# Filler on constant data from TensorE's first moment, smaller pieces of W_in, and a third bank for one slice, in a fused attention and MLP kernel

## The chip, the cores and the metric

One core of a Trainium2 chip. The metric is the device time of one execution in microseconds (us), median over runs; every run named here was fast, with a granted clock of 0.990 to 1.000. Times of a kernel come from up to five rounds, each beside runs of the kernel before on the same chip.

## The reference, cut to what matters

```python
# q, k, v: (4 batches, 8 heads, 768 positions, 64); blocks of 64 positions
intra = (qb @ kb.T * Dmask) @ vb                  # decayed attention in the block
inter = (qb * lam_pow) @ kv_state                 # what earlier blocks left
kv_state = lam_block * kv_state + (kb * rev_pow).T @ vb
...
h = x @ w_in                                      # x: attention output, (3072, 512); w_in (512, 2048)
g = np.where(h > 0.0, h, np.exp(np.minimum(h, 0.0)) - 1.0)
return g @ w_out                                  # w_out (2048, 512)
```

## The kernel before

The kernel works in chunks of 128 positions. A *group* is one chunk of one batch (24 groups), a *tile* of the MLP is up to four groups (512 tokens), and W_in is cut into 16 *slices* of 128 columns; slice n of tile t gives `psH`, which ScalarE reads twice (`e` is exp, `r` is relu) and VectorE turns into `g`. TensorE is the engine that counts; its instruction order is written by hand.

All loads in the part that matters are issued by GpSimd, one after the other, in the order of a list. Two entries in that list are no loads: `('kd', 0)` and `('kd', 2)` are multiplications of the keys by their decays, done by GpSimd between two issues.

```python
WI = [1, 1, 2, 2, 2, 4, 4]        # slices of W_in per transfer (128 KB each)
WO = [2, 2, 4, 4, 4]
...
LOADS = [(0, 1, 'q'), (0, 1, 'k'), ... (3, 1, 'v'),
         ('wi', 0), ('wi', 1), ('wi', 2), ('wi', 3), ('kd', 0),
         ('wi', 4), ('wi', 5), ('kd', 2), ('wo', 0), ('wi', 6),
         ('wo', 1), ('wo', 2), (4, 2), ('wo', 3), ('wo', 4), (6, 2), ...]
...
def run_loads(items):
    for it in items:
        if it[0] == "wi":   emit_wi(it[1])        # nc.gpsimd.dma_start(...)
        elif it[0] == "wo": emit_wo(it[1])
        elif it[0] == "kd": att_kd(it[1], 2, "p") # nc.gpsimd.tensor_tensor(...)
        else:               emit_load(*it)        # q, k, v of groups 4 and 5: (4, 2)
...
def mm1(t, n, alt=False):
    ...
    mm1_mm(t, n, 0, MT, "M" if t == 0 and n % 2 == 0 and n < 8 else "H")   # tag = which PSUM banks
...
def warm(k, tag="M"):             # filler: products whose results nobody reads
    for _ in range(k):
        nc.tensor.matmul(pw[:, 0:2], lhsT=ident16[:], rhs=any16[:, 0:2], start=True, stop=True)
any16 = ident16[:].unsqueeze(1).broadcast_to([128, 4, 128])
W = [10, 4, 3, 1, 2, 1, 2, 1, 3, 0, 0, 2, 0, 2, 0, 0, 3, 0, 0, 0]
...
visit(4, ('B', 1), ('B', 4), ('B', 7))   # group 4: its transposes of q and k come at step B1
```

Of the kernel before, what the change touches and what calls it, by code (L numbers as in the profile page):

```python
# [8 lines left out]
FP16 = mybir.dt.float16  # L9
# [6 lines left out]
def kernel(  # L16
# [27 lines left out]
    cpool = ctx.enter_context(tc.tile_pool(name="cst", bufs=1))  # L44
# [7 lines left out]
    nc.sync.dma_start(out=lam_b[:], in_=lam.unsqueeze(0).broadcast_to([128, H]))  # L52
    rel_i = cpool.tile([128, 128], I32, name="rel_i")


# [26 lines left out]

    WI = [1, 1, 2, 2, 2, 4, 4]
    WO = [2, 2, 4, 4, 4]
    wi_t, wo_t, wi_at, wo_at = [], [], {}, {}
    for i, w in enumerate(WI):
        for j in range(w):
# [7 lines left out]
    def emit_wi(i):  # L95
        f0 = sum(WI[:i]) * 128
        nc.gpsimd.dma_start(  # L97
            out=wi_t[i][:],
            in_=moe_w_in[:, f0 : f0 + WI[i] * 128].rearrange("(k p) f -> p k f", p=128),
        )  # L100

    def emit_wo(i):
        f0 = sum(WO[:i]) * 128
        nc.gpsimd.dma_start(
            out=wo_t[i][:],
            in_=moe_w_out[f0 : f0 + WO[i] * 128, :].rearrange("(n p) f -> p n f", p=128),
        )
# [4 lines left out]
    ]  # L112
    LOADS = [(0, 1, 'q'), (0, 1, 'k'), (1, 1, 'q'), (1, 1, 'k'), (2, 1, 'q'), (2, 1, 'k'), (3, 1, 'q'), (3, 1, 'k'), (0, 1, 'v'), (1, 1, 'v'), (2, 1, 'v'), (3, 1, 'v'), ('wi', 0), ('wi', 1), ('wi', 2), ('wi', 3), ('kd', 0), ('wi', 4), ('wi', 5), ('kd', 2), ('wo', 0), ('wi', 6), ('wo', 1), ('wo', 2), (4, 2), ('wo', 3), ('wo', 4), (6, 2), (8, 2), (10, 2), (12, 2), (14, 2), (16, 2), (18, 2), (20, 2), (22, 2)]

    def run_loads(items):
        for it in items:
            if it[0] == "wi":
                emit_wi(it[1])
            elif it[0] == "wo":
                emit_wo(it[1])  # L120
            elif it[0] == "kd":
                att_kd(it[1], 2, "p")
            else:
# [12 lines left out]
    ident16 = cpool.tile([128, 128], FP16, name="ident16")  # L136
# [64 lines left out]
    qT, kT, Pt, kds, xt, pT, pS = {}, {}, {}, {}, {}, {}, {}  # L201
# [230 lines left out]
    def mm1_mm(t, n, lo, hi, tag="H"):  # L432

        if n == 0 and lo == 0:
            gt[t] = msb.tile([128, NF, TS[t] * L], FP16, tag="g", bufs=2, name=f"g{t}")
        if lo == 0:
            pH_of[t, n] = ps.tile([128, TS[t] * L], FP32, tag=tag, bufs=2, name=f"psH{t}_{n}")
        pH = pH_of[t, n]
        wi, j = wi_t[wi_at[n][0]], wi_at[n][1]
        for kk in range(HP):  # L440
            nc.tensor.matmul(  # L441
                pH[:, lo:hi], lhsT=wi[:, kk, j * 128 : (j + 1) * 128],
                rhs=xt[t][:, kk, lo:hi], start=(kk == 0), stop=(kk == HP - 1),
            )

    def mm1(t, n, alt=False):

        MT = TS[t] * L
        if MT == 256:
            if n == 0:  # L450
                gt[t] = msb.tile([128, NF, MT], FP16, tag="g", bufs=2, name=f"g{t}")
            pH = ps.tile(
                [128, 2 * MT], FP32, tag="M" if (t, n) in ((1, 0),) else "H", bufs=2,
                name=f"psH{t}_{n}",
            )
            for x in range(2):
                wi, j = wi_t[wi_at[n + x][0]], wi_at[n + x][1]
                for kk in range(HP):
                    nc.tensor.matmul(  # L459
                        pH[:, x * MT : (x + 1) * MT],  # L460
                        lhsT=wi[:, kk, j * 128 : (j + 1) * 128],
                        rhs=xt[t][:, kk, :], start=(kk == 0), stop=(kk == HP - 1),
                    )
            MT *= 2
        else:
            if (t, n) not in pH_of:
                mm1_mm(t, n, 0, MT, "M" if t == 0 and n % 2 == 0 and n < 8 else "H")
            pH = pH_of.pop((t, n))
        e = msb.tile([128, MT], FP32, tag="e", bufs=3, name=f"e{t}_{n}")
        nc.scalar.activation(e[:], pH[:], AF.Exp)  # L470
        if alt:
            return e, None, pH
        r = msb.tile([128, MT], FP16, tag="r", bufs=3, name=f"r{t}_{n}")
        nc.scalar.activation(r[:], pH[:], AF.Relu)  # L474
        return e, r, pH
# [84 lines left out]
    def warm(k, tag="M"):  # L560
        if k <= 0:
            return
        pw = ps.tile([128, 4, 128], FP32, tag=tag, bufs=2, name=f"psW{len(warms)}")
        warms.append(pw)
        for _ in range(k):
            nc.tensor.matmul(  # L566
                pw[:, 0:2], lhsT=ident16[:], rhs=any16[:, 0:2], start=True, stop=True
            )

    warms = []  # L570
    pace = cpool.tile([1, 1], FP16, name="pace")
    any16 = ident16[:].unsqueeze(1).broadcast_to([128, 4, 128])

# [9 lines left out]
    def op_T(c, w):  # L583
        att_T(c, 1, w, "H")

    def op_Te(c, w):
        att_Te(c, 1, w, "a")

    W = [10, 4, 3, 1, 2, 1, 2, 1, 3, 0, 0, 2, 0, 2, 0, 0, 3, 0, 0, 0]
    warm(W[0])  # L590
    op_T(0, "q")
    op_Te(0, "q")
    build_mask0(1)
    warm(W[1])
# [12 lines left out]
    op_T(2, "q")
    op_Te(2, "q")
    att_S(1)
    att_mask(1, 2)  # L610
    warm(W[5])
    op_T(2, "k")
# [31 lines left out]

    run_loads(LOADS[16:28])
    for s, g in zip([], (0, 2)):
# [35 lines left out]
    def paced_load(s, items):  # L682

        t, n = s
        if t not in ("A", "B"):
            w = 2 if TS[t] == 2 else 1
            src = gt[t][0:1, n - w, 0:1] if n else gt[t - 1][0:1, NF - 1, 0:1]
            nc.gpsimd.tensor_copy(pace[:], src)  # L688
        run_loads(items)

    for s, a, b in [(('B', 2), 28, 29), ((1, 2), 29, 30), ((1, 14), 30, 31), ((2, 4), 31, 32), ((2, 12), 32, 33), ((3, 4), 33, 34), ((3, 12), 34, 35), ((4, 4), 35, 36)]:
        at(s, paced_load, s, LOADS[a:b])

# [51 lines left out]
```

## Time and profile before

| | before |
|---|---|
| time, median of 3 runs | 213.04 us (213.03 to 213.19) |
| span of the profiled run | 211.4 us |
| W_in slices 8 to 11 landed (512 KB) | 26.48 us |
| k of group 4 landed / its transposes start | 37.52 / 37.82 us |
| filler | 34 products |

First GpSimd's timeline (start, length, engine, line, operation, output<-inputs, count). The two `kd` lines are the stretches in which no load is issued.

```profile
14.95 2.04 POOL L295 TENSOR_TENSOR kd<-kn,ks 128x1024 f16<-128x1024 f16 x1
16.80 1.63 POOL L97 DMA_DIRECT2D wi<-in_moe_w_in_dram  x2
18.35 2.00 POOL L295 TENSOR_TENSOR kd<-kn,ks 128x1024 f16<-128x1024 f16 x1
20.20 0.79 POOL L104 DMA_DIRECT2D wo<-in_moe_w_out_dram  x1
```

Then busy time by stretch. Each row has the stretch and its length, the busy time of PE, PEld, DVE, ACT and POOL with counts, the granted clock, the DMA share, and as the last number the GB/s that the DMA engines moved.

```profile
20.00:21.50 1.50, 1.50 (x9) 0.68 (x7) 1.50 (x3) 1.22 (x4) 1.50 (x3) 1.00 1.04 133
21.50:23.00 1.50, 1.50 (x8) 0.49 (x6) 1.47 (x4) 1.46 (x3) 1.50 (x3) 1.00 1.14 180
23.00:24.00 1.00, 1.00 (x20) 0.64 (x20) 0.97 (x3) 0.89 (x2) 1.00 (x2) 1.00 1.14 124
24.00:26.50 2.50, 1.65 (x22) 0.72 (x20) 2.46 (x5) 1.88 (x4) 2.50 (x3) 1.00 1.20 195
26.50:30.50 4.00, 3.66 (x17) 1.61 (x18) 3.92 (x7) 2.76 (x6) 1.72 (x3) 1.00 1.24 206
```

### The profile page before, as it was taken

What the parts mean: (1) busy time and instruction counts of PE and PEld (TensorE: products, weight loads), DVE (VectorE), ACT (ScalarE), POOL (GpSimd) and SP (SyncE); (2) the same over time, 40 slices, a digit from 0 to 9 for tenths busy, and PEclk for the clock granted to TensorE, in tenths of its full rate; (3) what the DMA queues carried; (4) which work ended last, traced back from release to release, by engine and by line L of the source; (5) the groups of instructions that cost most, each with busy time, mean ns of one, the idle gap of its engine ahead of it and who ended that gap; (6) DMA issues with size and microseconds to landing.
All of it is one profiled execution on the core that took longest, in us unless ns stands there. A gap on an engine that the chain in (4) does not pass through costs nothing.

```text
span 211.4 us, 4157 instructions
## 1 busy us (share of the span) xinstructions
PE 203.4 (96%) x1654; PEld 108.0 (51%) x1654; DVE 147.6 (70%) x240; ACT 128.4 (61%) x247; POOL 61.5 (29%) x70
## 2 busy tenths in 40 slices
PE   5899899999999999999999999999999999999994
PEld 3664344556765454544544544544544544466643
DVE  6764995577989999998698598677557634344321
ACT  6779878406784858666464566474566476675620
POOL 8999955400434251250600500600000000011000
PEclk9999999999999999999999999999999999999999
DMA  5999999999999999999699991699401111011112
GB/s 36 142 159 176 174 204 164 201 157 182 227 142 140 136 171 163 118 104 108 118 146 153 105 126 55 113 148 155 83 0 53 50 50 50 5 50 50 50 53 101
DMA packets 100756, 24.40 MB, mean 115 GB/s; under 512 B 93056, under 2 KB 97920, under 8 KB 100736
## 3 DMA queue, kind: packets, MB, share of 16 engines
q0 software_dynamic: 80384, 14.16, 87.1%
q1 hardware_dynamic: 20208, 9.90, 22.0%
q8 instruction: 13, 0.21, 0.4%
q10 hardware_dynamic: 144, 0.07, 0.1%
q14 instruction: 7, 0.06, 0.1%
HBM read 27.27 MB, written 6.29 MB: 159 GB/s over the span
## 4 chain that ended last, share of the span: by engine, by line
PE 80%; POOL 8%; DMA 4%; DVE 3%; ACT 2%; issue 1%; POOLq 0%; ACTq 0%
PE psM L538 36%; PE psH L441 29%; PE psH L459 5%; DMA wi<-in_moe_w_in_dram 4%; PE psO L334 2%; PE psS L308 2%; PE psO L342 2%; POOL qn L72 2%; POOL wi L97 2%; POOL kn L72 2%; PE psM L518 2%; POOL vn L72 2%; DVE g L487 1%; ACT r L474 1%; DVE P L320 1%
## 5 line engine op out<-in xcount | busy, mean ns | idle before, releaser
L538 PE MATMUL psM<-wo,g 128*128 128x512 f16 x368 | 94.0, 380 | 0.2 <-DVE g L487 0.2
L470 ACT ACTIVATE e<-psH 128x512 f32<-128x512 f32 x96 | 57.3, 597 | 59.5 <-PE psH L441 50.8
L487 DVE SCALAR_TENSOR_TENSOR g<-e,r 128x512 f16<-128x512 f32 x93 | 63.5, 695 | 37.9 <-ACT r L474 37.6
L441 PE MATMUL psH<-xt,wi 128*128 128x512 f16 (+2 forms) x324 | 81.3, 376 | 1.5 <-DMA wi<-in_moe_w_in_dram 1.1
L474 ACT ACTIVATE r<-psH 128x512 f16<-128x512 f32 x93 | 55.1, 593 | 0.0
L538 PEld LDWEIGHTS <-g 128*128 128x128 f16 x368 | 34.3, 98 | 38.5 <-DVE g L487 1.5
L441 PEld LDWEIGHTS <-wi 128*128 128x128 f16 x324 | 31.1, 98 | 39.4 <-DMA wi<-in_moe_w_in_dram 1.7
L320 DVE TENSOR_TENSOR P<-psS,mask 128x1024 f16<-128x1024 f32 (+1 forms) x28 | 28.7, 1067 | 6.1 <-PE psS L308 6.0
L688 POOL COPY pace<-g 1x1 f16<-1x1 f16 x7 | 2.3, 329 | 68.8 <-DVE g L487 68.8
L418 DVE SCALAR_TENSOR_TENSOR st<-st,up_p,psU 64x128 f16<-64x128 f16 x64 | 18.2, 346 | 0.1
L555 POOL DMA_DIRECT2D out_dram<-osb x2 | 1.1, 571 | 54.8 <-ACT osb L554 50.7
L363 DVE TENSOR_TENSOR xt<-psO,qs 128x1024 f16<-128x1024 f32 x10 | 12.2, 1224 | 6.7 <-PE psO L342 6.7
L72 POOL DMA_DIRECT2D qn<-in_q_dram x14 | 15.4, 1099 | 4.2 <-issue 2.0
L459 PE MATMUL psH<-xt,wi 128*128 128x256 f16 x128 | 16.4, 273 | 0.0
L72 POOL DMA_DIRECT2D vn<-in_v_dram x14 | 15.2, 1104 | 2.1 <-DMA wo<-in_moe_w_out_dram 1.7
L72 POOL DMA_DIRECT2D kn<-in_k_dram x14 | 15.2, 1088 | 0.8 <-DMA kn<-in_k_dram 0.7
L459 PEld LDWEIGHTS <-wi 128*128 128x128 f16 x128 | 12.4, 98 | 4.2
L554 ACT COPY osb<-psM 128x512 f32<-128x512 f32 x12 | 7.1, 592 | 12.2 <-PE psM L538 12.2
L334 PEld LDWEIGHTS <-vn 128*64 128x64 f16 x184 | 9.5, 109 | 4.5 <-issue 4.4
L334 PE MATMUL psO<-P,vn 128*64 128x128 f16 x184 | 11.5, 222 | 0.1
L342 PE MATMUL psO<-qT,st 128*64 128x128 f16 x160 | 10.0, 219 | 0.0
L566 PE MATMUL psW<-ident 128*128 128x256 f16 x34 | 8.3, 372 | 1.6 <-DVE ident L140 1.6
(58 smaller groups left out, 119.7 us busy)
## 6 DMA issues: line engine op xcount, KB each, us to landing
out_dram<-osb SPq DMA_DIRECT2D x21, 256.0 KB, 2.3
qn<-in_q_dram POOLq DMA_DIRECT2D x10, 256.0 KB, 6.7
kn<-in_k_dram POOLq DMA_DIRECT2D x10, 256.0 KB, 7.8
vn<-in_v_dram POOLq DMA_DIRECT2D x10, 256.0 KB, 9.4
wo<-in_moe_w_out_dram POOLq DMA_DIRECT2D x3, 512.0 KB, 14.9
wi<-in_moe_w_in_dram POOLq DMA_DIRECT2D x2, 512.0 KB, 9.1
wi<-in_moe_w_in_dram POOLq DMA_DIRECT2D x3, 256.0 KB, 6.3
qn<-in_q_dram POOLq DMA_DIRECT2D x4, 128.0 KB, 4.6
```

The costliest lines, as they stand in the source:

```text
L72: nc.gpsimd.dma_start(out=dst, in_=src[b : b + n, :, rows].rearrange("b h p d -> p (b h) d"))
L320: nc.vector.tensor_tensor(out=P[:, :, c], in0=s[:, :, c], in1=(mask if g < B else mask1)[:, :, c], op=ALU.mult,)
L334: nc.tensor.matmul(po[r, i, hp, :], lhsT=v_of(g + i, 2 * hp + hh), rhs=P[:, hh, hp, :], start=True, stop=(c == 0), skip_group_check=True,)
L342: nc.tensor.matmul(po[r, i, hp, :], lhsT=st[(g + i) % B // 2][c % 2][:, (g + i) % 2, hp, r], rhs=qT[g + i][:, hp, :], start=False, stop=Tr ...
L363: nc.vector.tensor_tensor(out=dst, in0=po[:, :, c], in1=qs[:, c].unsqueeze(1).broadcast_to([128, n, w, 128]), op=ALU.mult,)
L418: nc.vector.scalar_tensor_tensor(out=new[r, :, hp, r], in0=old[r, :, hp, r], scalar=up_p[r, hp : hp + 1], in1=pu[r, :, hp, :], op0=ALU.mul ...
L441: nc.tensor.matmul(pH[:, lo:hi], lhsT=wi[:, kk, j * 128 : (j + 1) * 128], rhs=xt[t][:, kk, lo:hi], start=(kk == 0), stop=(kk == HP - 1),)
L459: nc.tensor.matmul(pH[:, x * MT : (x + 1) * MT], lhsT=wi[:, kk, j * 128 : (j + 1) * 128], rhs=xt[t][:, kk, :], start=(kk == 0), stop=(kk = ...
L470: nc.scalar.activation(e[:], pH[:], AF.Exp)
L474: nc.scalar.activation(r[:], pH[:], AF.Relu)
L487: nc.vector.scalar_tensor_tensor(out=g, in0=e[:], scalar=-1.0, in1=r[:], op0=ALU.add, op1=ALU.min)
L538: nc.tensor.matmul(pm[:], lhsT=gt[t][:, n, i * L : (i + 1) * L], rhs=wo_t[wo_at[n][0]][:, wo_at[n][1], :], start=(n == 0), stop=(n == NF - 1),
```

## The change

Its intent: (a) get TensorE out of its slow opening sooner, with filler that does not wait for the identity and with more of it; (b) let slices 8 and 9 of W_in arrive without waiting for 10 and 11; (c) let slice 10 not wait for the bank of slice 8. Cut to its core:

```diff
+    ones = cpool.tile([128, 128], FP16, name="ones")
+    nc.vector.memset(ones[:], 1.0)
-    WI = [1, 1, 2, 2, 2, 4, 4]
+    WI = [1, 1, 2, 2, 2, 2, 2, 4]
     LOADS = [...
-      ('kd', 0), ('wi', 4), ('wi', 5), ('kd', 2), ('wo', 0), ('wi', 6), ('wo', 1), ...
+      ('kd', 0), ('wi', 4), ('wi', 5), ('kd', 2), ('wi', 6), ('wo', 0), ('wi', 7), ('wo', 1), ...
-  mm1_mm(t, n, 0, MT, "M" if t == 0 and n % 2 == 0 and n < 8 else "H")
+  mm1_mm(t, n, 0, MT, "M" if t == 0 and n % 2 == 0 and n < 9 else "H")
-  pw[:, 0:2], lhsT=ident16[:], rhs=any16[:, 0:2], start=True, stop=True
+  pw[:, 0:2], lhsT=ones[:], rhs=any16[:, 0:2], start=True, stop=True
-    any16 = ident16[:].unsqueeze(1).broadcast_to([128, 4, 128])
+    any16 = ones[:].unsqueeze(1).broadcast_to([128, 4, 128])
-    W = [10, 4, 3, 1, 2, 1, 2, 1, 3, 0, 0, 2, 0, 2, 0, 0, 3, 0, 0, 0]
+    W = [18, 7, 3, 2, 3, 1, 2, 2, 4, 0, 0, 3, 0, 3, 0, 0, 4, 0, 0, 0]
```

(The rest shifts indices into the list of loads by one and adds a branch that is never taken.)

More of the change, by code (lines that the diff above doesn't have):

```diff
@@ L112 @@
     ]
-    LOADS = [(0, 1, 'q'), (0, 1, 'k'), (1, 1, 'q'), (1, 1, 'k'), (2, 1, 'q'), (2, 1, 'k'), (3, 1, 'q'), (3, 1, 'k'), (0, 1, 'v'), (1, 1, 'v'), (2, 1, 'v'), (3, 1, 'v'), ('wi', 0), ('wi', 1), ('wi', 2), ('wi', 3), ('kd', 0), ('wi', 4), ('wi', 5), ('kd', 2), ('wo', 0), ('wi', 6), ('wo', 1), ('wo', 2), (4, 2), ('wo', 3), ('wo', 4), (6, 2), (8, 2), (10, 2), (12, 2), (14, 2), (16, 2), (18, 2), (20, 2), (22, 2)]
+    LOADS = [(0, 1, 'q'), (0, 1, 'k'), (1, 1, 'q'), (1, 1, 'k'), (2, 1, 'q'), (2, 1, 'k'), (3, 1, 'q'), (3, 1, 'k'), (0, 1, 'v'), (1, 1, 'v'), (2, 1, 'v'), (3, 1, 'v'), ('wi', 0), ('wi', 1), ('wi', 2), ('wi', 3), ('kd', 0), ('wi', 4), ('wi', 5), ('kd', 2), ('wi', 6), ('wo', 0), ('wi', 7), ('wo', 1), ('wo', 2), (4, 2), ('wo', 3), ('wo', 4), (6, 2), (8, 2), (10, 2), (12, 2), (14, 2), (16, 2), (18, 2), (20, 2), (22, 2)]
     def run_loads(items):
@@ L643 @@
             ecut[x[1]] = cut[x[1]]
-    run_loads(LOADS[16:28])
+    run_loads(LOADS[16:29])
     for s, g in zip([], (0, 2)):
@@ L688, in paced_load @@
             nc.gpsimd.tensor_copy(pace[:], src)
+        elif 6 in kds:
+            nc.gpsimd.tensor_copy(pace[:], kds[6][0:1, 0, 0:1])
         run_loads(items)
-    for s, a, b in [(('B', 2), 28, 29), ((1, 2), 29, 30), ((1, 14), 30, 31), ((2, 4), 31, 32), ((2, 12), 32, 33), ((3, 4), 33, 34), ((3, 12), 34, 35), ((4, 4), 35, 36)]:
+    for s, a, b in [(('B', 2), 29, 30), ((1, 2), 30, 31), ((1, 14), 31, 32), ((2, 4), 32, 33), ((2, 12), 33, 34), ((3, 4), 34, 35), ((3, 12), 35, 36), ((4, 4), 36, 37)]:
         at(s, paced_load, s, LOADS[a:b])
```

## The prediction

> **What bounds the kernel now.** I read the page of the profile first: the engine table, then the chain of work that ended last.
>
> ```profile
> PE 203.4 (96%) x1654; PEld 108.0 (51%) x1654; DVE 147.6 (70%) x240; ACT 128.4 (61%) x247; POOL 61.5 (29%) x70
> PE 80%; POOL 8%; DMA 4%; DVE 3%; ACT 2%; issue 1%; POOLq 0%; ACTq 0%
> L566 PE MATMUL psW<-ident 128*128 128x256 f16 x34 | 8.3, 372 | 1.6 <-DVE ident L140 1.6
> ```
>
> TensorE is busy 96% of a 211.4 us span and carries 80% of the chain. The chain's other 20% is where a change of the opening can work: GpSimd 8% and DMA 4% are the first 26.5 us, in which the chain is the issue of the loads and then the landing of one piece of W_in. The filler of today is 34 products of 128x256; the first waits 1.6 us for the identity.
>
> Then the timeline of the opening, matmuls only, for who waits for what and for the clock that TensorE really has:
>
> ```profile
> 1.65 2.31 PE L566 MATMUL psW<-ident 128*128 128x256 f16 x10 [1.65 <-DVE ident L140]
> 4.91 0.61 PE L221 MATMUL psTq<-ident,qn 128*128 128x128 f16 x4 [0.95 <-DMA qn<-in_q_dram]
> 7.07 0.61 PE L221 MATMUL psTk<-ident,kn 128*128 128x128 f16 x4 [0.70 <-DMA kn<-in_k_dram]
> ...
> 10.83 0.61 PE L308 MATMUL psS<-qT,kT 64*128 64x128 f16 x8
> 12.97 0.40 PE L308 MATMUL psS<-qT,kT 64*128 64x128 f16 x8
> ...
> 17.21 2.06 PE L441 MATMUL psH<-xt,wi 128*128 128x384 f16 x12
> ...
> 19.45 3.63 PE L441 MATMUL psH<-xt,wi 128*128 128x512 f16 x16 [0.18 <-DMA wi<-in_moe_w_in_dram]
> ...
> 26.53 1.90 PE L441 MATMUL psH<-xt,wi 128*128 128x512 f16 x8 [0.88 <-DMA wi<-in_moe_w_in_dram]
> 28.74 1.02 PE L441 MATMUL psH<-xt,wi 128*128 128x512 f16 x4 [0.31 <-ACT r L474]
> ```
>
> Columns: start, length, engine, line, output<-inputs, count, and the wait before it. The same eight products take 0.61 us at 10.83 and 0.40 us at 12.97: TensorE is slow until about 12.9 us, although the page's granted clock reads 1.00 throughout. From 17.2 us on, the stretches without a product running are only these (a product counted as its 216 ns start-to-start): 0.15 at 18.03, 0.34 at 19.45 (slices 2 and 3 of W_in), 1.05 at 26.53 (slices 8 and 9), 0.48 at 28.74 (slice 10 waits for ACT to read slice 8 out of its bank), 0.27 at 67.2, 0.34 at 93.9. Sum 2.6 us. All else after 17.2 is solid TensorE work that the change leaves alone. **So the change can win 2 us at the very most, under 1%.**
>
> **What the Trainium skill says.** "TensorE: Matmul & The Clock Gate", Part 1: the clock is at half rate by default and is released after about 3.4 us of sustained matmul activity, seen through a free-running window. The trace agrees: filler products start 0.21 us apart at first, 0.11 us apart after 13.3 us; two idle stretches (0.95 and 0.70 us) came before. "DMA: Bandwidth & Descriptors", "Why a DMA increments its semaphore by 16 and not by 1": a DMA has landed only when the slowest of 16 engines is done. That fits a queue busy at 90% or more from 5 us on, with 6 to 16 us from issue to landing. "PSUM — Partial Sum Buffer", Specifications: 8 banks of 512 FP32, so one 128x512 slice fills a bank; this kernel's three tags hold 4, 2 and 2 banks, as its tile shapes show.
>
> **The change, part by part.** The order of instructions: TensorE gains 36 rows (18 matmuls and their weight loads), VectorE one memset ahead of everything, GpSimd one W_in transfer. The new branch in the pacing of loads is never taken (no new GpSimd copy).
>
> (a) *Filler from the first moment.* 34 become 52 products. Its data come from a 128x128 memset (about 0.1 us, estimated from the 0.23 us of a 128x128 VectorE operation here) that waits for nothing, so filler starts near 0.9 us. 18 x 0.213 = 3.8 us reaches 4.75, just short of the first q at 4.91; 7 x 0.213 = 1.5 us fills 5.3 to 6.9, just short of k at 7.07. TensorE is then busy from 0.9 us without a break, and should be fast somewhere between 4.5 and 8 us instead of 12.9. Filler never delays data: at the full clock the 2 to 4 products per step are 0.2 to 0.45 us against 0.9 us per arriving load. Each score group (S) saves 0.2 us and each transpose 0.2 us, so TensorE follows the arrivals. Working through them (last k at 12.5, last v at 16.1 us), the last output group of the first tile moves from 16.87 to about 16.1, and slice 0 from 17.21 to about 16.55 us: **0.65 us earlier. But none of it reaches the end by itself:** slices 2 and 3 start at 19.45 because their transfer (issued 13.46, 5.9 us to landing) lands at 19.4, and GpSimd's issues don't depend on TensorE. It becomes a longer wait at 19.45.
>
> (b) *W_in in two-slice pieces.* Today slices 8 to 11 are one 512 KB transfer, issued at 17.59 and landed 8.9 us later, at 26.48; the piece before landed at 23.11. The new 256 KB piece for 8 and 9 should land about halfway, 24.8 us (estimate), before TensorE wants it at 25.5. The 1.05 us wait goes. Slices 10 and 11 are now issued after a 2.0 us multiplication on GpSimd (kd, 18.35 to 20.35), at about 20.2 instead of 17.59; the queue still holds two pieces then, so I put them at 26.5 as before, against a need at 27.2.
>
> (c) *Slice 8 in a third bank.* Slices 8, 9, 10 share two banks today, so 10 waits for the reading of 8. With 8 in a bank of the other tag (free since slice 4 was read, 24.4 us), 10 needs the bank of 7, free at 26.4. The 0.48 us wait goes; slice 11 now waits for slice 9's reading instead, to about 28.7 against a start of 30.03 today.
>
> Sum of (b) and (c): slice 11 about 1.3 us earlier. **Then it is given back**, since the loads behind are not earlier. Landings today (issue plus time to landing) against use:
>
> - W_in slices 12 to 15: landed 30.31, used 31.33: slack 1.0
> - W_out slices 2 and 3: landed 31.59, used 32.19: 0.6
> - W_out slices 4 to 7: landed 34.13, used 34.78: 0.65
> - k of group 4: landed 37.52, transposed at 37.82: 0.3
> - W_out slices 8 to 11: landed 41.70, used about 42.4: 0.7
>
> TensorE runs in order, so the smallest slack caps the gain: 0.3 us, if these transfers land as before. After 42 us every slack is over 1 us and TensorE is solid, so what is left goes through to the end: about 0.3 us.
>
> **The rivals.**
> 1. *Transfers land earlier too.* From 20 to 21.5 and 23 to 24 us the queue moved only 133 and 124 GB/s, against 195 to 206 just after. The 512 KB piece took 3.4 us after its predecessor where the next 512 KB took 2.5. If the smaller piece heals that, everything behind lands up to 0.8 us earlier, and the gain is up to 1.1 us: 211.9.
> 2. *Transfers land later.* With 256 KB less in the queue while GpSimd multiplies, the queue may run dry, and 256 KB pieces move at about 184 GB/s (17 to 20 us) against 206 for 512 KB ones, which alone costs 512 KB x (1/184 - 1/206) = 0.3 us. Then k of group 4 lands after today's use and the change costs 0 to 0.5 us: up to 213.5.
> 3. *Filler in the way.* If the clock isn't released earlier, 18 more products at 0.213 us are 3.8 us of TensorE, 11 of them before 7 us in idle time, the other 7 (1.5 us) in a stretch that today is solid. Slice 0 would then start near 18.7 and slice 2 about 1 us late. Against it: TensorE would be busy without a break, more than what released it before. I give it 1 in 20.
>
> **Range and chances.** The core is 213.04 - 0.3 = 212.75 us; rival 1 seems to me likelier than rival 2, because today's dips came with the large piece, so I take 212.5. Range 211.7 to 213.4: from rival 1 with a little more to rival 2. 2% would be 4.3 us, more than all gaps together. Faster 0.01, same 0.98, slower 0.01.
>
> **What would show it.** The first filler near 0.9 us; score groups of 0.40 us from the first or second on; slice 0 near 16.6; slices 2 and 3 still at 19.4 with a wait near 1 us; slice 8 near 25.5 without a wait; slice 11 near 28.7; then new short waits for DMA between 30 and 38 us, the last before the transposes of group 4; from 40 us on, the same timeline shifted by one constant. I am wrong if the landings between 23 and 38 us shift by more than 0.8 us either way, if the clock stays slow past 9 us, or if some later wait (ACT, VectorE around 57 to 67 us) swallows the shift.

## The result, and the profile after

| | before | after |
|---|---|---|
| time, median of 6 runs each | 213.07 us (212.82 to 213.19) | 213.62 us (213.24 to 213.89) |
| ratio | | 1.0026, 95% interval 1.0013 to 1.0039 |
| span of the profiled run | 211.4 us | 211.4 us |

The ratio is the mean time of one kernel's fast runs over that of the other's of the same rounds, so not quite the ratio of the medians. The change costs 0.26%, about 0.55 us: "same" at a threshold of 2%, but slower, and 0.2 us above the predicted range.

The engines are as busy as before (PE 203.4 us in both). What differs is the chain (the first line, from the page after; the second is the group of the filler):

```profile
PE 75%; POOL 11%; DMA 6%; DVE 3%; ACT 2%; issue 1%; POOLq 0%; ACTq 0%
L568 PE MATMUL psW<-ones 128*128 128x256 f16 x52 | 9.6, 325 | 1.1 <-DVE ones L55 1.1
```

TensorE's part fell from 80% to 75%; GpSimd's rose from 8% to 11% and DMA's from 4% to 6%. The filler starts 0.6 us sooner (1.06 us against 1.65) and its products are shorter in the mean (325 ns instead of 372). The same chain in order of time (start, length, what) names the stretch:

```profile
18.44 1.93 POOL kd L297
20.37 0.69 POOL wi L99
21.05 0.71 POOL wo L106
...
25.19 12.56 DMA kn<-in_k_dram
37.79 0.62 PE psT L223 x8
```

The end of the program now hangs on k of group 4, on its way from 25.19 to 37.75 us, and that load on GpSimd, whose own multiplication of 1.93 us is a link of the chain. TensorE's timeline after, to be laid beside the prediction's:

```profile
1.06 4.02 PE L568 MATMUL psW<-ones 128*128 128x256 f16 x18 [1.06 <-DVE ones L55]
4.98 0.40 PE L223 MATMUL psTq<-ident,qn 128*128 128x128 f16 x4
...
16.80 0.41 PE L336 MATMUL psO<-P,vn 128*64 128x128 f16 x8 [1.74 <-DMA vn<-in_v_dram]
...
18.03 5.48 PE L443 MATMUL psH<-xt,wi 128*128 128x384 f16 x28
...
26.02 2.76 PE L443 MATMUL psH<-xt,wi 128*128 128x512 f16 x12
...
32.32 1.02 PE L443 MATMUL psH<-xt,wi 128*128 128x512 f16 x4 [0.37 <-ACT r L476]
```

TensorE is at full speed (four transposes in 0.40 us) at 4.98 us instead of 12.97. The 12 products at 26.02 are slices 8, 9 and 10 in one run, so the waits of 1.05 and 0.48 us are gone. Two new waits have come, for v at 16.80 and for ScalarE at 32.32. And the transposes of k start at 37.79, 0.04 us after its load has landed, after a gap of 0.28 us.

This profile is of the *fastest* of the change's six runs (213.24 us). A second profile, of experiment e15 (the change unedited, a run of 213.95 us), shows a run of the slow end, with its waits for loads:

```profile
30.45 1.04 PE L443 MATMUL psH<-xt,wi 128*128 128x512 f16 x4 [0.34 <-DMA wi<-in_moe_w_in_dram]
32.23 0.59 PE L540 MATMUL psM<-wo,g 128*128 128x512 f16 x2 [0.75 <-DMA wo<-in_moe_w_out_dram]
...
38.50 0.62 PE L223 MATMUL psT<-ident,kn 128*128 128x128 f16 x8 [0.48 <-DMA kn<-in_k_dram]
```

And busy time by stretch after, to be laid beside that of before:

```profile
20.00:21.50 1.50, 1.50 (x8) 0.69 (x7) 0.94 (x2) 1.50 (x4) 1.50 (x3) 1.00 1.39 184
21.50:23.00 1.50, 1.50 (x9) 0.68 (x7) 1.47 (x4) 1.40 (x4) 1.50 (x3) 1.00 1.22 158
23.00:24.00 1.00, 1.00 (x20) 0.45 (x19) 1.00 (x3) 0.85 (x2) 1.00 (x2) 1.00 1.12 137
24.00:26.50 2.50, 2.50 (x27) 1.17 (x26) 2.45 (x5) 1.98 (x5) 2.50 (x4) 1.00 1.02 130
26.50:30.50 4.00, 4.00 (x20) 1.72 (x19) 3.89 (x7) 3.48 (x7) 2.71 (x4) 1.00 1.20 197
```

The dip at 20 us has healed (133 to 184), but a longer one has come at 24 to 26.5 us (195 to 130). Rate times length, summed from 20 to 30.5 us: 1905 KB before, 1763 KB after, so 142 KB less; the stretch from 17 to 20 us gives 24 KB back (184 against 192 GB/s). The 118 KB that remain are 0.6 us at some 200 GB/s, the size of the loss. These rates are of one execution each and differ between executions; which part of them comes back in every profile is tabled after e16.

**A constant of this kernel.** In the profiles of before, after, e1 to e10, e12, e13, e15 and e16, the time from the start of the transposes of k of group 4 to the end of the span is 173.6 to 173.7 us. So in these profiles the run time is set by when those transposes start, and every experiment can be read at that one point. (e11 and e14 change what comes after it and have 173.4 and 172.8.)

**How the load gets there.** A load has landed when the last of 16 DMA engines is done. The traces hold 16 landing times for each load, without the engine's number; in order of time, for k of group 4:

| | 8th engine done | last engine done | transposes start |
|---|---|---|---|
| before | 35.44 | 37.52 | 37.82 |
| after, first profile | 37.07 | 37.75 | 37.79 |
| after, second profile (e15) | 36.68 | 38.45 | 38.50 |

In these two profiles the eighth engine is 1.2 to 1.6 us later after the change. The last one, which decides, is only 0.2 to 0.9 us later, since it lagged 2.1 us behind the eighth before; that it still had work where the others ran out is a guess. How far the last engine lags differs from run to run, so the eighth engine is the steadier witness. Much of the spread between runs may come from the last one: in the two profiles of the change k landed 0.70 us apart, and their times lie 0.71 us apart.

### The profile page after: what moved, and what is told of

It reads as the page before. It is cut to its first block, busy times and chain, and to the rows that moved or that the text cites. A ratio compares the mean times of both kernels' runs of the same rounds, so it can differ in the third digit from the quotient of the medians.

```text
span 211.4 us, 4194 instructions
## 1 busy us (share of the span) xinstructions
PE 203.4 (96%) x1672; PEld 107.8 (51%) x1672; DVE 147.5 (70%) x241; ACT 128.1 (61%) x247; POOL 62.4 (29%) x71
## 4 chain that ended last, share of the span: by engine, by line
PE 75%; POOL 11%; DMA 6%; DVE 3%; ACT 2%; issue 1%; POOLq 0%; ACTq 0%
PE psM L540 34%; PE psH L443 26%; DMA kn<-in_k_dram 6%; PE psH L461 5%; POOL wi L99 3%; PE psO L336 2%; PE psS L310 2%; POOL qn L74 2%; PE psO L344 2%; POOL kd L297 2%; POOL kn L74 2%; PE psM L520 2%; POOL vn L74 2%; DVE g L489 1%; DVE P L322 1%; ACT kd L295 1%
## 5 line engine op out<-in xcount | busy, mean ns | idle before, releaser
L322 DVE TENSOR_TENSOR P<-psS,mask 128x1024 f16<-128x1024 f32 (+1 forms) x28 | 28.7, 1067 | 5.0 <-PE psS L310 4.9
L74 POOL DMA_DIRECT2D kn<-in_k_dram x14 | 15.2, 1084 | 1.5 <-DMA kn<-in_k_dram 0.9
L74 POOL DMA_DIRECT2D vn<-in_v_dram x14 | 15.2, 1102 | 1.2 <-DMA wo<-in_moe_w_out_dram 1.1
L568 PE MATMUL psW<-ones 128*128 128x256 f16 x52 | 9.6, 325 | 1.1 <-DVE ones L55 1.1
```

The source lines that it names most:

```text
L74: nc.gpsimd.dma_start(out=dst, in_=src[b : b + n, :, rows].rearrange("b h p d -> p (b h) d"))
L322: nc.vector.tensor_tensor(out=P[:, :, c], in0=s[:, :, c], in1=(mask if g < B else mask1)[:, :, c], op=ALU.mult,)
```

## The experiments

Theories, as the quoted expectations name them. **A**: the added filler, through its instructions, costs the time. **B**: the W_in pieces and their place in the list of loads do. Within B, **S**: the load queue starves (moves fewer bytes than it could) because GpSimd multiplies instead of issuing, with fewer bytes issued ahead of it; **P**: small pieces are slow in themselves. All sixteen runs gave correct results.

### e1: the filler alone

```diff
 # before, plus only: ones, memset, lhsT=ones, any16 from ones, and
+    W = [18, 7, 3, 2, 3, 1, 2, 2, 4, 0, 0, 3, 0, 3, 0, 0, 4, 0, 0, 0]
```

> The filler part alone on the kernel before. Theory A (the loss is in the filler's instructions: 36 more rows on TensorE make the 16 KB instruction packet come at 14.7 us instead of 16.7, one DMA engine is late by a microsecond and the last two v pieces land near 16.8 and 17.1 instead of 15.3 and 16.1): slice 0 starts at 17.8 to 18.2, the wait of 1 us for the 512 KB W_in piece near 26 us stays, end 0.3 to 0.8 us slower than before. Theory B (the loss is in the W_in pieces, filler is harmless): slice 0 starts at 16.6, slices 2 and 3 at 19.4, end within 0.15 us of before.

Measured: median 212.94 us against 212.94; ratio 1.0016 (0.9978 to 1.0053), with one run at 215.25 and the others from 212.41 to 213.10. The filler costs nothing that can be seen, though with that one run the interval alone would allow a loss of the change's size; e2 decides. Its profile has the wait ahead of slices 2 and 3 grown to 0.84 us (at 19.52), so it also gains nothing, as the prediction said of part (a).

### e2: the pieces and the bank, with the old filler

```diff
 # before, plus only: WI, LOADS and n < 9 of the change
```

> W_in in two-slice pieces and slice 8 in the third bank, with the filler of before. Theory A: instruction packet at 16.7 us as before, v lands as before, slice 0 at 17.2, slice 8 without a wait near 25.5, end 0.2 to 0.6 us faster than before (held back by VectorE near 31 us and by k of group 4 near 37.5). Theory B: k of group 4 lands at 37.8 or later because of the smaller pieces, end 0.2 to 0.6 us slower than before.

Measured: 213.67 us against 212.94; ratio 1.0033 (1.0020 to 1.0047). The whole loss, without the filler. In its profile the transposes wait for k:

```profile
38.21 0.62 PE L221 MATMUL psT<-ident,kn 128*128 128x128 f16 x8 [1.18 <-DMA kn<-in_k_dram]
```

### e3: the pieces alone

```diff
 # before, plus only: WI and LOADS of the change
```

> The W_in pieces alone, slice 8 in its old bank. Theory A: as the run with the bank, but slice 10 waits for the reading of slice 8, so between before and that run: 0.0 to 0.4 us faster than before. Theory B: slower than before by 0.2 to 0.6 us, and equal to the run with the bank within 0.15 us.

Measured: 213.61 us; ratio 1.0032 (1.0019 to 1.0046); k of group 4 landed at 38.46, with the eighth engine at 36.61. So the loss is in (b) alone.

### e4: the change with half as many, twice as wide filler products

```diff
-        for _ in range(k):
+        for w in [4] * (k // 2) + [2] * (k % 2):
-                pw[:, 0:2], lhsT=ones[:], rhs=any16[:, 0:2], start=True, stop=True
+                pw[:, 0:w], lhsT=ones[:], rhs=any16[:, 0:w], start=True, stop=True
```

> The whole change, its filler in half as many products of twice the width: 29 products instead of 52, the same columns and the same time on TensorE. Theory A: the instruction packet comes at 16 to 17 us again, the v pieces land near 15.3 and 16.1, slice 0 at 16.6, end 0.3 to 0.8 us faster than the whole change. Theory C (dense filler itself, not its instructions, delays the loads): v lands near 16.8 as in the change, end within 0.15 us of the change (0.3 to 0.8 us slower than before).

Measured: 213.40 us; ratio 1.0024 (1.0009 to 1.0039). Theory A's mechanism shows in part: a 16 KB packet of instructions for TensorE moved from 14.7 us (after) to 16.3 (e4; before: 16.7), and the last two v loads landed at 15.2 and 15.87 instead of 16.75 and 17.05. (With the packet at 13.75 in e1 and 14.12 in e15 the last v landed at 16.35 and 16.57, so how late v is differs between executions.) But the time stayed: k landed at 38.03. A is refuted as the cause of the loss.

### e5: the piece for slices 10 and 11 ahead of the multiplication

```diff
-  ('wi', 4), ('wi', 5), ('kd', 2), ('wi', 6), ('wo', 0), ...
+  ('wi', 4), ('wi', 5), ('wi', 6), ('kd', 2), ('wo', 0), ...      # on the kernel after
```

> The whole change, but the piece for slices 10 and 11 is issued ahead of GpSimd's second kd multiplication, as its bytes were before. Theory S (the queue runs dry: 256 KB less is queued while GpSimd multiplies for 2 us): k of group 4 lands at 37.2 to 37.6 as before or earlier, end 0.0 to 0.5 us faster than before. Theory P (two 256 KB pieces with 512 B packets are slower than one 512 KB piece with 1024 B packets, wherever they stand): k of group 4 lands at 37.7 to 38.4 as in the change, end 0.3 to 0.8 us slower than before.

Measured: 213.25 us against 212.89; ratio 1.0011 (0.9970 to 1.0052). This has the same bytes issued ahead of the multiplication as the kernel before, in smaller pieces. Rates of 190, 191 and 176 GB/s from 20 to 24 us, but 176 and 185 from 24 to 30.5, since W_out's first piece is now issued at 20.96 instead of 20.20: one more issue takes GpSimd 0.75 us. The eighth engine was done with k at 36.14, the last at 37.21. Part of the loss seems gone; the interval does not prove it, and the medians (0.36 us slower) fit neither theory's expectation.

### e6 and e7: the multiplication behind the loads

```diff
-  ('wi', 5), ('kd', 2), ('wi', 6), ('wo', 0), ('wi', 7), ('wo', 1), ('wo', 2), (4, 2), ...
+  ('wi', 5), ('wi', 6), ('wo', 0), ('wi', 7), ('wo', 1), ('wo', 2), ('kd', 2), (4, 2), ...   # e6, on after
 # e7: the same move on before
```

> The whole change, with the second kd multiplication only after the last W_out piece has been issued. Theory S: the low rates of the queue between 21 and 27 us go, k of group 4 lands at 36.5 to 37.2, end 0.3 to 0.9 us faster than before. Theory P: k of group 4 at 37.7 or later, end as the change.

> The kernel before with nothing changed but the place of the second kd multiplication, after the last W_out piece of the opening. Theory S: the low rates at 20 to 24 us go, k of group 4 lands at 36.5 to 37.2, end 0.3 to 0.8 us faster than before. Theory P: the low rates have another cause and stay, end within 0.15 us of before.

Measured: e6 215.99 us, ratio 1.0129 (1.0090 to 1.0169); e7 214.16, ratio 1.0066 (1.0029 to 1.0103). Both much slower, against expectation: a miss. The rates did heal in e7 (182, 176, 155, 193 GB/s where before had 133, 180, 124, 195), so the link between the multiplication and the dips holds. The time went elsewhere, into VectorE. Lines of three engines of e6:

```profile
20.74 3.88 DVE L489 SCALAR_TENSOR_TENSOR g<-e,r 128x512 f16<-128x512 f32 x1 [0.29 <-ACT r L476]
22.02 2.04 POOL L297 TENSOR_TENSOR kd<-kn,ks 128x1024 f16<-128x1024 f16 x1
26.18 1.89 PE L443 MATMUL psH<-xt,wi 128*128 128x512 f16 x8 [2.51 <-DVE g L487]
```

One VectorE operation that takes 0.69 us elsewhere took 3.88 us, until 0.56 us after the end of GpSimd's; TensorE then waited 2.51 us. So these two runs do not test what later landings cost. For this kernel the multiplication has to leave GpSimd's list *and*, in this stretch, must not run beside VectorE's operations.

### e8: less issued ahead of the multiplication, with large pieces

```diff
-  ('kd', 0), ('wi', 4), ('wi', 5), ('kd', 2), ('wo', 0), ...
+  ('kd', 0), ('wi', 4), ('kd', 2), ('wi', 5), ('wo', 0), ...      # on before: the 512 KB piece behind kd
```

> The kernel before with nothing changed but that the 512 KB piece (slices 8 to 11) is issued after the second kd multiplication. Theory S: all 512 KB are missing from the queue, twice what the change took out, so k of group 4 lands at 38.2 to 39.2, end 0.7 to 1.5 us slower than before. Theory P: no small pieces, so k of group 4 lands at 37.5 to 37.7; slice 8 waits longer near 27 us, end within 0.3 us of before.

Measured: 214.16 us against 212.89; ratio 1.0049 (1.0014 to 1.0084); k landed at 38.25 with the eighth engine at 36.34. No piece was made smaller, only the amount ahead of the multiplication, and the rate fell deeper than anywhere:

```profile
20.00:21.50 1.50, 1.50 (x7) 0.68 (x8) 0.53 (x2) 1.47 (x3) 1.50 (x3) 1.00 0.80 81
```

The lower rate and the later landings are as S expected, in a kernel where P has nothing to say. The time is not a clean test: the moved piece itself landed later (27.01 us instead of 26.48), slice 8 waited for it until 27.05 instead of 26.53, and this 0.52 us is all that the transposes of k are late in the profile (38.34 against 37.82).

### e9 and e10: the multiplication on VectorE, in a stretch where it idles

```diff
-  ('wi', 5), ('kd', 2), ...          # taken out of LOADS
-    run_loads(LOADS[16:29])
+    run_loads(LOADS[16:28])
+    att_kd(2, 2, "v")                # e10, on after; e9: the same on before
```

> The kernel before with the second multiplication of the keys by the decays moved from GpSimd to VectorE, into a stretch where VectorE idles. Theory S (the load queue runs dry while GpSimd multiplies, because GpSimd also issues the loads): the low rates between 20 and 24 us vanish, k of group 4 lands at 36.5 to 37.2 us instead of 37.52, and the end comes 0.0 to 0.6 us before the kernel before, as far as TensorE can use it. Theory P (the size of the pieces sets the rate): the landing stays within 0.2 us of 37.5 and the time within 0.15 us.

> The changed kernel with the same multiplication moved to VectorE. Theory S: k of group 4 lands at 36.4 to 37.2 us, its transposes start at 37.1 to 37.5 us limited by TensorE or VectorE, and the end comes 0.2 to 0.6 us before the kernel before, 0.8 to 1.2 us before the changed kernel's median. Theory P (small pieces are slow in themselves): the landing stays at 37.7 us or later and the time within 0.2 us of the changed kernel's.

Measured, on one chip: e9 213.00 us against 212.98, ratio 0.9998 (0.9979 to 1.0017); e10 212.80 us, ratio 0.9987 (0.9967 to 1.0006). On VectorE the multiplication took 1.22 us (17.67 to 18.89). In this profile of e10 the dips are nearly gone:

```profile
20.00:21.50 1.50, 1.50 (x8) 0.68 (x7) 1.21 (x3) 1.21 (x4) 1.50 (x3) 1.00 1.38 183
21.50:23.00 1.50, 1.50 (x8) 0.59 (x6) 1.26 (x3) 1.50 (x3) 1.50 (x2) 1.00 1.33 178
23.00:24.00 1.00, 1.00 (x20) 0.61 (x20) 0.97 (x3) 0.85 (x3) 1.00 (x2) 1.00 1.40 199
24.00:26.50 2.50, 2.50 (x27) 1.16 (x26) 2.46 (x5) 1.98 (x4) 2.42 (x4) 1.00 1.23 201
```

The eighth engine was done with k at 35.53 and the last at 36.56; the transposes started at 36.66, and the chain's DMA part fell to 3%, with TensorE at 84%. The pieces are the change's small ones, and the eighth engine is level with that of e9 (35.46), which has the large one; so P is refuted. e9 shows that the same move is worth nothing measurable in the kernel before: its k landed at 36.99, as S expected, but its eighth engine was at 35.46 as before (35.44), so those engines had lost nothing there with 256 KB more issued ahead of the multiplication, and waits ahead of slices 8 and 10 remained (0.44 us, now with ScalarE as the releaser, and 0.48 us). Its runs fell into two clusters, 212.48 to 212.69 and 213.31 to 213.36; why is open.

### e11: group 4 one step later

```diff
-  visit(4, ('B', 1), ('B', 4), ('B', 7))
+  visit(4, ('B', 2), ('B', 5), ('B', 8))      # on after
```

> The changed kernel with the stages of group 4 one step later in TensorE's order, loads untouched. If the landing of k of group 4 is what holds the changed kernel back, the wait ahead of its transposes goes and the end comes 0.3 to 0.9 us before the changed kernel (212.7 to 213.3 us against a kernel before of 213.0). If something else holds it, the time stays within 0.15 us of 213.6.

Measured: 213.09 us, ratio 0.9997 (0.9979 to 1.0015), so about level with before instead of 0.26% behind. The loads are untouched (eighth engine 36.69); only TensorE's need for k was moved back. This agrees, from the other side, with k's landing being what the change lost its time to.

### e12: a delay of GpSimd, without smaller pieces

```diff
             elif it[0] == "kd":
                 att_kd(it[1], 2, "p")
+                if it[1] == 2:
+                    nc.gpsimd.iota(pad_i[:], pattern=[[1, 640]], base=0, channel_multiplier=-1)   # on before
```

> The kernel before with one more small instruction on GpSimd right after its second multiplication, meant to take about 0.8 us, which is the time of one more load issue, with W_in's pieces as before. Theory S (GpSimd's time ahead of the next issue is what counts): k of group 4 lands 0.3 to 0.8 us later, and the end comes 0.2 to 0.7 us later. Theory P (small pieces): landing and time within 0.15 us of the kernel before.

Measured: 213.18 us against 212.98; ratio 1.0014 (0.9996 to 1.0032). The extra instruction took 0.75 us and the next issue came 0.64 us later (20.84); the eighth engine was 0.24 us later (35.68), and k's landing was not later at all (37.45). Inconclusive, and weaker than S had it: 0.75 us more of GpSimd costs little while 256 KB more are queued ahead. That the bytes ahead count for more than the extra issue is a reading of this run, not shown: e5, with the bytes of before ahead and one more issue, has its eighth engine 0.7 us later than before, and no run says why that is more than here.

### e13 to e16: the change, its repair, and two variants on one chip

```diff
 # e15: the kernel after, unedited
 # e16: e10 again
 # e13: e10 with the old filler (ident16, old W)
 # e14: e10 with group 4 one step later, as in e11
```

> The changed kernel unedited, on the same chip as the two repairs. Expected: slower than the kernel before by 0.3 to 0.8 us, as in the first measurement, with k of group 4 landing after 37.5 us and its transposes waiting for it.

> The change with the second multiplication on VectorE once more, as the yardstick for the three others on one chip. Theory S expects it 0.5 to 1.0 us before the changed kernel and 0.1 to 0.5 us before the kernel before; theory P, no difference from the changed kernel.

> The two-slice pieces, the third bank and the second multiplication on VectorE, but with the old filler: what is the new filler worth once the loads no longer hold the end? If it is worth something, TensorE is late after its cold start and the end comes 0.3 to 0.6 us later than with the new filler (same chip). If slices 2 and 3 wait for their landing at 19.5 us in either case, as the prediction said, the two agree within 0.15 us.

> The best version so far (the whole change, second multiplication on VectorE) with group 4's stages one step later. In the profile of the version without this step TensorE had hardly a wait left between 20 and 60 us, so at most 0.1 to 0.3 us can be gained: 0.3 to 0.9 us before the kernel before. If the landing of k of group 4 still varies between runs and holds some of them, the spread of its runs also becomes smaller.

| against before (212.89 us, 11 runs) | median us | lowest to highest | ratio, 95% interval | 8th / last engine done with k |
|---|---|---|---|---|
| e15, the change | 213.56 | 213.19 to 213.95 | 1.0034 (1.0015 to 1.0053) | 36.68 / 38.45 |
| e16, multiplication on VectorE | 212.49 | 212.15 to 212.88 | 0.9986 (0.9967 to 1.0004) | 35.52 / 37.34 |
| e13, as e16 with the old filler | 212.83 | 212.26 to 213.51 | 0.9997 (0.9976 to 1.0019) | 35.38 / 38.01 |
| e14, as e16 with group 4 later | 212.35 | 212.03 to 213.28 | 0.9982 (0.9958 to 1.0005) | 35.60 / 37.58 |

The slowest run of e16 is faster than the fastest of e15: moving one 2 us instruction off GpSimd is worth 1.07 us in the medians, the whole loss and 0.4 us more. So the loss needs the multiplication between GpSimd's issues, as S says; how it divides between fewer bytes ahead and one more issue is not shown. The new filler may be worth something once the loads allow it (e16 against e13, 0.34 us in the medians), but the intervals overlap widely; that is not shown. In e14 the smaller spread that was expected did not come (1.25 us from lowest to highest, e16 0.73). e14 was the best version run, 0.5 us below before in the medians, and its interval just reaches 1, as do those of e10 and e16; no version is proven faster than the kernel before.

What comes back in all profiles of a kind, one profile per run:

| | 8th engine done with k | GB/s from 24 to 26.5 us |
|---|---|---|
| loads as before, multiplication on GpSimd (before, e1) | 35.44, 35.72 | 195, 197 |
| loads of the change, multiplication on GpSimd (after, e2, e3, e4, e11, e15) | 36.26 to 37.07 | 130 to 167 |
| loads of the change, multiplication on VectorE (e10, e13, e14, e16) | 35.38 to 35.60 | 193 to 201 |

Other dips do not come back: the one at 20 us (133 GB/s) is 173 in e1, with the same loads, and e16, the kernel of e10, has 149 from 21.5 to 23 us.

## Why the prediction was wrong, step by step

- **Bound and ceiling: right.** TensorE's busy time did not change, and everything lay in the opening.
- **(a), the clock: right.** The first filler came at 1.06 us (I said 0.9), and TensorE was fast at 4.98 us (I said 4.5 to 8). TensorE was not "busy from 0.9 us without a break", though: the fast filler ran out and it waited 0.97 us for k at 7.12, but stayed fast. **Slice 0 at 16.55: wrong**; it came at 18.03 and 17.20. I let TensorE follow the arrivals of before (last v at 16.1), but the last v landed at 17.05 and 16.57, and slice 0's piece at 17.72 and 17.15. In the first profile the packet with TensorE's instructions came 2 us earlier, among the v loads; with fewer filler products (e4) it came late again. (The "6 to 16 us from issue to landing" were misread too: the first loads take 3.5 to 5.) As predicted, none of this reached the end: the filler alone cost and gained nothing that can be seen (e1), and the loss is whole without it (e2).
- **(b) and (c) at their own place: right.** Slices 8 and 9 landed at 23.8 (I said 24.8), 10 and 11 at 26.2 (I said 26.5), and both waits are gone. Slice 11 started at 29.20 and, in e15, 28.66 (I said 28.7).
- **A wait that I had not seen.** In the first profile slice 13 waits at 32.32 (a gap of 0.53 us). VectorE, busy with the state copy at 28.99 (1.38 us), was behind, and one of the three `e` buffers was not free. It took back most of the 0.8 us that had been gained up to slice 11, down to 0.3 us.
- **The step that failed: "the smallest slack caps the gain: 0.3 us, if these transfers land as before", and the choice of rival 1 over rival 2.** I had the slack at k of group 4 as the binding one, which was right; the term that was mis-sized is its landing. I put it at 37.52 or, in rival 1, up to 0.8 us earlier; the profiles have it at 37.75 and 38.45. In the first, TensorE had been ready 0.28 us before its transposes started. In e15 two landings ahead of it, W_in 12 to 15 at 30.40 (before 30.31) and W_out 2 and 3 at 32.19 (before 31.59), had already taken back the 1.4 us gained up to slice 11, and k then cost 0.65 us more. Such waits between 30 and 38 us, the last before k, were forecast; that they would take more than the gain was not. I wrote of slices 10 and 11 that "the queue still holds two pieces then", and checked only that piece. What came in its place: with 256 KB less issued ahead of the multiplication (1.3 us of moving at 195 GB/s) the loads *behind* that piece were late, the eighth engine at k by 0.5 to 1.6 us, and without the multiplication on GpSimd they were not (35.38 to 35.60).
- **The argument for rival 1 was the wrong reading of a right observation.** I put the dips at 20 and 23 us down to the large piece "because today's dips came with" it. They came some 5 us after GpSimd's two multiplications (14.95 and 18.35) just as well. The dip at 20 us did not even come back in e1 (173) and e12 (184), with the large piece; the one at 23 us did (120 and 141). e8, with the large piece kept and less ahead of the multiplication, had the deepest (81 GB/s), and with the multiplication on VectorE the change had 162 to 199 at 23 us. Nor was there much to heal: in e9, with 176 at 23 us, the eighth engine was no earlier at k. Rival 2 named the cause, the multiplication with 256 KB less in the queue, and its end ("up to 213.5", which the stated range to 213.4 cut short; measured 213.62); its other half, that small pieces cost 0.3 us by themselves, fell with e10.
- **Rival 3, filler in the way: not seen** (e1).

What stays open: why so few bytes moved in the dip. Loads were not lacking: from 24 to 26.5 us of the profile after, W_in 12 to 15 and W_out 2 to 7 (issued from 21.72 to 24.05) were still under way, so "runs dry" is not shown in that sense. By the packet records there were fewer packets of 512 bytes or more (348, against 503 in e10), each as short as there (median 0.098 us in both), but 12 of them took over 0.3 us (one in e10); what the engines waited for no record says. Open too: why one engine lags by up to 2 us, and by how much in which run; and what the filler is worth in e16.

## What to carry to other kernels

Where an engine both computes and issues loads, count the bytes already issued when it starts to compute; cutting a transfer in two with the computation between its halves takes from exactly that. Here 256 KB less ahead, with one more issue behind, cost some 0.6 us, and moving the computation to another engine brought that back. Before shortening a wait on the bound engine, list the next loads with their slack and ask what the change does to *their* issue time, not only to that of the piece that was cut. A dip in the DMA rate can come from what the issuing engine did some 5 us earlier, as here, and not from the transfer that is moving in it; and compare several executions before reading one dip, since not every dip comes back.

## What the Trainium skill lacked or had wrong

- "SBUF — State Buffer", "Who interferes with whom", says that a VectorE instruction with two SBUF inputs contends with a GpSimd instruction that reads SBUF, and that the one that issues second is blocked until the first is done. e6 and e7 agree in that VectorE was held (3.88 us for an operation of 0.69 us in e6, 4.83 us for two in e7). But the record of the held operation starts 1.3 us *before* that of GpSimd's multiplication in e6 (20.74 against 22.02; at 0.69 us it would have been done at 21.43) and ends 0.56 us after it, so the order of the records does not show who blocks; the page does not say how this looks in a profile.
- "TensorE: Matmul & The Clock Gate", "Part 1", has full speed after some 3.4 us of sustained matmul activity. The trace agrees: full speed no later than 3.9 us after the first filler (1.06 to 4.98 us). What it lacks is that the profile page's row of granted clock does not show this gate: it reads 9 tenths or more in all 40 slices of both kernels, also where products take 0.61 us instead of 0.40 us.
- "DMA: Bandwidth & Descriptors", "Why a DMA increments its semaphore by 16 and not by 1", says that the slowest of 16 engines decides. It lacks the size of the lag: 2.1 us between the eighth and the last engine at k of group 4 before, 0.7 and 1.8 us in the two profiles of the change.
- The pages that I read have no number for how long loads from GpSimd's list last once GpSimd computes: here a stretch of 1.8 us without an issue (18.4 to 20.2 us) came back as a dip some 5 us later, deeper or longer with fewer bytes issued ahead of it (124 GB/s for 1 us before, 130 GB/s for 2.5 us after the change).
